# Two key tiles per PV matmul, and head selection folded into the transposes, in a decode attention kernel

## Chip, core and metric

The kernel runs on one core of a Trainium2 chip. The metric is the device time of one execution, in microseconds (us). The engines are called by the profile's names: PE is TensorE (matmuls), PEld its weight loads, DVE is VectorE, ACT is ScalarE, POOL is GpSimd, SP is SyncE, which here only issues DMAs. The core has 16 DMA engines. Times within a run are counted from the start of its span.

## The reference, cut to what matters

Two independent attention blocks, A and B, each decode one token for a batch of 2 with 32 heads of width 192 over a cache of 8192 keys. All tensors are bf16.

```python
q = (x @ wq).reshape(B, Sq, H, Dh).transpose(0, 2, 1, 3)      # B=2, Sq=1, H=32, Dh=192
scores = einsum("bhqd,bhkd->bhqk", q, k_cache) * Dh ** -0.5   # k_cache: 2 x 32 x 8192 x 192
p = softmax(scores)
o = einsum("bhqk,bhkd->bhqd", p, v_cache)
out = o.transpose(0, 2, 1, 3).reshape(B, Sq, H * Dh) @ wo     # A and B are concatenated
```

Every key and value is read once: 2 blocks x 2 x 32 = 128 (batch, head) items, each with 3 MB of keys and 3 MB of values. An item is called a head below, numbered 0 to 127; 16 of them (8 heads x batch 2) form a group, and there are 8 groups.

## The kernel before

For each head, SP loads keys into one of 2 slots and values into one of 3. A key slot is free when VectorE has multiplied it, a value slot when the PV of its head (probabilities times values) is done:

```python
                if i >= NK:
                    sp.wait_ge(s_mul, NCH * (i - NK + 1))
                sp.dma_start(
                    kslot(i % NK), kc[b, h].rearrange("(p t) d -> p (t d)", p=P)
                ).then_inc(s_k[i % NK], 16)
                if i >= NV:
                    sp.wait_ge(s_pv, i - NV + 1)
                sp.dma_start(
                    vslot(i % NV), vc[b, h].rearrange("(p t) d -> p (t d)", p=P)
                ).then_inc(s_v[i % NV], 16)
```

VectorE multiplies keys by the broadcast query in four chunks; PE sums the products by multiplying with an identity matrix (24 matmuls of 512 columns per head); VectorE finishes the sum, ACT takes the exponential, and PE multiplies the probabilities with the values. The weights of the PV matmul are a window of 16 columns into a row of zeros with the probabilities of this head in the middle, so that the head lands in its own row of a 16-row accumulator:

```python
            def pv_quarter(i, c):
                blk, g, m, hh, b, h = item(i)
                if c == 0:
                    pe.wait_ge(s_exp, i + 1)
                    pe.wait_ge(s_v[i % NV], 16 * (i // NV + 1))
                    if m == 0:
                        pe.wait_ge(s_zero, g + 1 if g >= 2 else 2)
                zs = zwin_slot(i % 2)
                vv = vslot(i % NV).rearrange("p (t d) -> p t d", d=Dh)
                tq = T // NCH
                for t in range(c * tq, (c + 1) * tq):
                    pe.matmul(
                        O_ps[g % 2][0:G, 0:Dh],
                        lhsT=zs[:, t, G - 1 - m:2 * G - 1 - m],
                        rhs=vv[:, t, :],
                        start=False, stop=False, skip_group_check=True,
                    )
                if c == NCH - 1:
                    pe.matmul(
                        O_ps[g % 2][0:G, Dh:Dh + 1],
                        lhsT=rz_slot(i % 2)[:, G - 1 - m:2 * G - 1 - m],
                        rhs=ones_f[:, 0:1],
                        start=False, stop=False, skip_group_check=True,
                    ).then_inc(s_pv, 1)
```

VectorE starts the multiplies of head i+1 before it has finished head i, and PE places a quarter of the PV of head p-1 after each reduction chunk of head p:

```python
# VectorE
            for i in range(NH):
                nxt = i + 1 < NH
                # [cut]
                if nxt:
                    mul_chunk(i + 1, 0)
                sred_nrs(i)
                if nxt:
                    mul_chunk(i + 1, 1)
                bias_op(i)
                # [cut: group end] then chunks 2 and 3
# TensorE
            for p in range(NH + 1):
                for c in range(NCH):
                    if p < NH:
                        red_chunk(p, c)
                    if p >= 1:
                        pv_quarter(p - 1, c)
                if p < NH:
                    pe.wait_ge(s_nrs, p + 1)
                    pe.transpose(
                        out=MT_ps[:, 0:P],
                        in_=nrs[:, (p % 2):(p % 2) + 1].broadcast_to([P, P]),
                        identity=ident_f[:, :],
                    ).then_inc(s_maxt, 1)
```

At the end of a group the 16 rows are normalized, spread out 8 times, transposed in bf16, masked so that each row keeps only its own head, and multiplied with `wo`. After the last group of a block the 16 rows are added up by head with an fp32 selection matmul:

```python
            def group_end(g):
                ops = O_ps[g % 2]
                dve.wait_ge(s_pv, G * (g + 1))
                dve.reciprocal(out=rcp[:, :], in_=ops[0:G, Dh:Dh + 1]).then_inc(s_rcp, 1)
                dve.wait_ge(s_rcp, g + 1)
                if g >= 1:
                    dve.wait_ge(s_ot, g)
                dve.tensor_scalar(
                    out=o_rep[:, :].rearrange("m (j h q) -> m j h q", j=NJ, h=HG),
                    in0=ops[0:G, 0:Dh].rearrange("m (q j) -> m j q", j=NJ)[:, :, None, :].broadcast_to([G, NJ, HG, DQ]),
                    scalar1=rcp[:, 0:1], scalar2=None, op0=ALU.mult,
                ).then_inc(s_onorm, 1)
                dve.wait_ge(s_onorm, g + 1)
                dve.memset(ops[0:G, 0:Dh + 1], 0.0).then_inc(s_zero, 1)

            def mask_copy(g):
                dve.wait_ge(s_ot, g + 1)
                if g >= 1:
                    dve.wait_ge(s_proj, NPP * g)
                dve.tensor_tensor(
                    out=oM_sb[:, :].rearrange("p (j m) -> p j m", m=G),
                    in0=aux_ps[:, 0:NJ * G].rearrange("p (j m) -> p j m", m=G),
                    in1=mask_b[:, None, :].broadcast_to([P, NJ, G]),
                    op=ALU.mult,
                ).then_inc(s_mc, 1)
# [cut]
            def out_transposes(g, p):
                pe.wait_ge(s_onorm, g + 1)
                pe.wait_ge(s_qc, q_count_before(p + 1))
                if g >= 1:
                    pe.wait_ge(s_mc, g)
                for j in range(NJ):
                    tr = pe.transpose(
                        out=aux_ps[:, j * G:(j + 1) * G],
                        in_=o_rep[:, j * P:(j + 1) * P],
                        identity=ident_b[0:G, 0:G],
                    )
                tr.then_inc(s_ot, 1)
```

Of the kernel before, what the change touches and what calls it, by code (L numbers as in the profile page):

```python
# [5 lines left out]
BF16 = mybir.dt.bfloat16  # L6
# [6 lines left out]
def bass_concat_heads__gqa_block_cached__mha_block_cached__decode_kernel(  # L13
# [28 lines left out]
    W = 2 * G - 1  # L42
# [48 lines left out]

    proj_sched = {}
    for g in range(NG):
        for q in range(NPP):
            p = min((g + 1) * G + 1 + q, NH)
            proj_sched.setdefault(p, []).append((g, q))
    acc_sched = {}
    for blk in range(NBLK - 1):
        gl = (blk + 1) * NGB - 1
        acc_sched[(gl + 1) * G + NPP] = blk  # L100
# [6 lines left out]
    for g in range(1, NG):  # L107
        sp_extra.setdefault(g * G + 7, []).append(("wo", g))

    es = contextlib.ExitStack()  # L110
    with es:
# [12 lines left out]
        zwin = sb("zwin", [P, 2 * T * W], BF16)  # L124
        rz = sb("rz", [P, 2 * W], F32)
# [7 lines left out]
        ones_b = sb("ones_b", [P, G], BF16)  # L133
        mask_b = sb("mask_b", [P, G], BF16)
        sel_f = sb("sel_f", [G, Bsz], F32)
        x_sb = sb("x_sb", [Bsz, NBLK * D], BF16)
        xT = sb("xT", [P, NBLK * DC * Bsz], BF16)
        o_rep = sb("o_rep", [G, NJ * P], BF16)
        rcp = sb("rcp", [G, 1], F32)
        oM_sb = sb("oM_sb", [P, NJ * G], BF16)  # L140
        acc_sb = sb("acc_sb", [G, D], F32)
        out_sb = sb("out_sb", [Bsz, NBLK * D], BF16)
# [3 lines left out]
        MT_ps = banks[2]  # L146
        O_ps = [banks[3], banks[4]]
# [24 lines left out]
        s_rcp = sem("s_rcp")  # L172
        s_onorm = sem("s_onorm")
# [4 lines left out]
        s_accc = sem("s_accc")  # L178
        s_sel = sem("s_sel")
# [17 lines left out]
        def zwin_slot(j):  # L197
            return zwin[:, j * T * W:(j + 1) * T * W].rearrange("p (t w) -> p t w", w=W)

        def rz_slot(j):  # L200
            return rz[:, j * W:(j + 1) * W]

# [17 lines left out]
        def _(pool):  # L220
            pool.memset(ident_f[:, :], 1.0).then_inc(s_pl, 1)
            pool.memset(ones_b[:, :], 1.0).then_inc(s_pl, 1)
# [5 lines left out]
            mview = mask_b[:, :].rearrange("p (h b) -> p h b", b=Bsz)  # L228
            oview = ones_b[:, :].rearrange("p (h b) -> p h b", b=Bsz)
            pool.affine_select(  # L230
                out=mview, in_=oview, pattern=[[-DQ, HG], [0, Bsz]],
                compare_op=ALU.is_ge, fill=0.0, base=0, channel_multiplier=1,
            ).then_inc(s_pl, 1)
            pool.wait_ge(s_pl, 4)
            pool.tensor_copy(out=ident_b[:, :], in_=ident_f[:, :]).then_inc(s_pl, 1)
            pool.affine_select(
                out=mview, in_=mview, pattern=[[DQ, HG], [0, Bsz]],
                compare_op=ALU.is_ge, fill=0.0, base=DQ - 1, channel_multiplier=-1,
# [4 lines left out]
            pool.wait_ge(s_pl, 9)  # L243
# [3 lines left out]
        def _(sp):  # L247
# [5 lines left out]
            for i in range(NH):  # L253
                blk, g, m, hh, b, h = item(i)
                _, kc, vc, _, _ = blocks[blk]
                for (kind, gg) in sp_extra.get(i, []):
# [3 lines left out]
                    else:  # L260
                        if gg >= 1:
                            sp.wait_ge(s_proj, NPP * gg)
                        load_wo(sp, gg)
                if i >= NK:
                    sp.wait_ge(s_mul, NCH * (i - NK + 1))
# [11 lines left out]
            sp.dma_start(out.rearrange("b o n -> b (o n)"), out_sb[:, :]).then_inc(s_out, 16)  # L277
            sp.wait_ge(s_out, 16)

        @block.vector  # L280
        def _(dve):
            dve.memset(O_ps[0][0:G, 0:Dh + 1], 0.0)
            dve.memset(O_ps[1][0:G, 0:Dh + 1], 0.0).then_inc(s_zero, 2)
            dve.wait_ge(s_const, 1)
            dve.tensor_reduce(
                out=sel_f[:, :], in_=ident_f[0:G, 0:G].rearrange("p (h b) -> p b h", b=Bsz),
                axis=AX.X, op=ALU.add,
            ).then_inc(s_dc, 1)
            qc_waited = [0]

# [43 lines left out]
            def group_end(g):  # L334
                ops = O_ps[g % 2]
                dve.wait_ge(s_pv, G * (g + 1))
                dve.reciprocal(out=rcp[:, :], in_=ops[0:G, Dh:Dh + 1]).then_inc(s_rcp, 1)
                dve.wait_ge(s_rcp, g + 1)
                if g >= 1:
                    dve.wait_ge(s_ot, g)  # L340
                dve.tensor_scalar(  # L341
                    out=o_rep[:, :].rearrange("m (j h q) -> m j h q", j=NJ, h=HG),
                    in0=ops[0:G, 0:Dh].rearrange("m (q j) -> m j q", j=NJ)[:, :, None, :].broadcast_to([G, NJ, HG, DQ]),
                    scalar1=rcp[:, 0:1], scalar2=None, op0=ALU.mult,
                ).then_inc(s_onorm, 1)
                dve.wait_ge(s_onorm, g + 1)
                dve.memset(ops[0:G, 0:Dh + 1], 0.0).then_inc(s_zero, 1)  # L347

            def mask_copy(g):
                dve.wait_ge(s_ot, g + 1)  # L350
                if g >= 1:
                    dve.wait_ge(s_proj, NPP * g)
                dve.tensor_tensor(  # L353
                    out=oM_sb[:, :].rearrange("p (j m) -> p j m", m=G),
                    in0=aux_ps[:, 0:NJ * G].rearrange("p (j m) -> p j m", m=G),
                    in1=mask_b[:, None, :].broadcast_to([P, NJ, G]),
                    op=ALU.mult,
                ).then_inc(s_mc, 1)

            for c in range(NCH):  # L360
                mul_chunk(0, c)
            for i in range(NH):
                nxt = i + 1 < NH
                ge = i >= 1 and (i - 1) % G == G - 1
                if nxt:
                    mul_chunk(i + 1, 0)
                sred_nrs(i)
                if nxt:
                    mul_chunk(i + 1, 1)
                bias_op(i)  # L370
                if ge:
                    group_end((i - 1) // G)
                if nxt:
                    mul_chunk(i + 1, 2)
                if ge:
                    mask_copy((i - 1) // G)
                if nxt:
                    mul_chunk(i + 1, 3)
            group_end(NG - 1)
            mask_copy(NG - 1)  # L380

        @block.scalar
        def _(act):
# [15 lines left out]
            def acc_copy(blk):  # L399
                gl = (blk + 1) * NGB - 1  # L400
                act.wait_ge(s_proj, NPP * (gl + 1))
                if blk >= 1:
                    act.wait_ge(s_sel, blk)
# [198 lines left out]
```

## Time and profile before

| | before |
|---|---|
| median of 4 runs | 1996.02 us (1995.7 to 1998.07) |
| the profiled run | span 1994.0 us |
| HBM read | 836.8 MB |

These are lines of the page of the kernel before: the engines' busy time with its share of the span, the queue of the data loads (q1) and of the instruction loads (q8) with packets, megabytes and the share of the 16 DMA engines' time, the chain of waits, and the costliest groups (busy time and mean ns of one; then the engine's idle time before them, and who ended it).

```profile
span 1994.0 us, 26935 instructions
...
PE 1668.2 (84%) x12274; PEld 1019.3 (51%) x12274; DVE 1016.3 (51%) x1059; ACT 99.5 (5%) x330; POOL 5.0 (0%) x14
...
q1 hardware_dynamic: 43276, 836.79, 98.4%
q8 instruction: 97, 1.59, 0.3%
...
DMA 71%; DVE 19%; issue 7%; PE 2%; ACT 0%; SPq 0%; ACTq 0%; DVEq 0%
...
L303 DVE TENSOR_TENSOR pbuf<-kbuf,qbc 128x3072 bf16<-128x3072 bf16 x512 | 886.9, 1752 | 941.7 <-DMA kbuf<-in_A_k_cache_dram 478.8
L476 PE MATMUL bank<-pbuf,ident_b 128*128 128x512 bf16 x3072 | 812.2, 404 | 0.2 <-DVE pbuf L303 0.2
L495 PE MATMUL bank<-vbuf,zwin 128*16 128x192 bf16 x8192 | 786.1, 251 | 23.8 <-ACT zwin L422 19.4
```

The q1 row is the one that matters: the loads keep the 16 DMA engines busy for 98.4% of the span, and the chain that ended last is 71% key loads. VectorE's idle time before the multiplies is spent waiting for keys.

The second view is the timeline of the tail, which is what is left to do once the last keys are in; the time up to there is called the steady part below (start, duration, engine, line and operation; in brackets the idle time before it). The last keys are in when the first multiply of head 127 starts.

```profile
1960.93 1.76 DVE L303 TENSOR_TENSOR pbuf<-kbuf,qbc 128x3072 bf16<-128x3072 bf16 x1 [6.79 <-DMA kbuf<-in_B_k_cache_dram]
...
1974.83 0.69 DVE L312 TENSOR_REDUCE sc_sb<-bank 128x64 f32<-128x512 f32 x1 [5.96 <-PE bank L476]
...
1977.55 5.45 PE L495 MATMUL bank<-vbuf,zwin 128*16 128x192 bf16 x64 [1.05 <-ACT zwin L422]
...
1983.06 0.16 DVE L337 RECIPROCAL rcp<-bank 16x1 f32<-16x1 f32 x1 [6.24 <-PE bank L502]
1983.25 1.80 DVE L341 TENSOR_SCALAR o_rep<-bank,rcp 16x1536 bf16<-16x1536 f32 x1
...
1985.11 0.45 PE L515 MATMUL bank<-ident_b,o_rep 16*128 16x16 bf16 x12 [2.09 <-DVE o_rep L341]
...
1986.01 0.38 PE L534 MATMUL bank<-wo_sb,oM_sb 128*16 128x512 bf16 x1 [0.44 <-DVE oM_sb L353]
...
1989.21 0.22 PE L535 MATMUL bank<-wo_sb,oM_sb 128*16 128x128 bf16 x1
...
1991.53 0.59 ACT L409 ACTIVATE out_sb<-bank 2x512 bf16<-2x512 f32 x1 [1.32 <-PE bank L542]
...
1992.30 0.27 SPq L277 DMA_DIRECT2D out_dram<-out_sb  x1
```

From the last keys (1960.93) to the last scores (1974.83) 13.9 us pass, then exponential and PV, then from 1983.06 the group end: the spreading takes 1.80, the 12 transposes 0.45, the projection 3.4 (1986.01 to 1989.43), and 2.1 us go by until the output copy can start (1991.53): they are the copy and the selection matmuls of the block's end.

### The profile page before, as it was taken

To read this page: it belongs to the slowest core of one execution; us is meant where nothing else is said; L and a number is where in the kernel's file an instruction comes from. 1 tells how busy PE (TensorE), PEld (TensorE's weight loads), DVE (VectorE), ACT (ScalarE), POOL (GpSimd) and SP (SyncE) were. 2 spreads that over 40 slices of the span, in tenths; PEclk is the share of its full clock that TensorE was granted. 3 is DMA by queue.
4 is the path that set the end of the run, shared out by engine and by line. 5 is a ranking of instruction groups with operands and counts; after the bars stand their busy time and mean duration, and the time that the engine had idled before them with its cause. 6 is when DMAs were issued, how large, how long until landed. Compare 5 with 4: busy or idle time off the path is not lost.

```text
span 1994.0 us, 26935 instructions
## 1 busy us (share of the span) xinstructions
PE 1668.2 (84%) x12274; PEld 1019.3 (51%) x12274; DVE 1016.3 (51%) x1059; ACT 99.5 (5%) x330; POOL 5.0 (0%) x14
## 2 busy tenths in 40 slices
PE   6868879788888888878888888787888878987887
PEld 2545545455555555545555455454555545554455
DVE  3545455445554555445455455554455545554543
ACT  0000000000000000000000000000000000000000
POOL 0000000000000000000000000000000000000000
PEclk8989999899998999999999999998998999999999
DMA  9999999999999999999999999999999999999993
GB/s 402 425 432 430 429 427 430 428 430 430 426 430 429 430 430 426 428 431 427 430 426 428 428 428 425 424 428 430 428 428 424 423 431 429 425 414 429 430 431 165
DMA packets 43389, 838.51 MB, mean 421 GB/s; under 512 B 4358, under 2 KB 4362, under 8 KB 9484
## 3 DMA queue, kind: packets, MB, share of 16 engines
q1 hardware_dynamic: 43276, 836.79, 98.4%
q8 instruction: 97, 1.59, 0.3%
q14 instruction: 16, 0.13, 0.0%
HBM read 836.77 MB, written 0.01 MB: 420 GB/s over the span
## 4 chain that ended last, share of the span: by engine, by line
DMA 71%; DVE 19%; issue 7%; PE 2%; ACT 0%; SPq 0%; ACTq 0%; DVEq 0%
DMA kbuf<-in_A_k_cache_dram 37%; DMA kbuf<-in_B_k_cache_dram 35%; DVE pbuf L303 15%; DVE sc_sb L312 2%; PE bank L495 1%; PE bank L476 1%; DVE ns_sb L320 1%; DVE o_rep L341 1%; DVE bias L329 1%; PE bank L534 0%; DVE bank L347 0%; DVE oM_sb L353 0%; PE bank L541 0%; ACT zwin L422 0%; PE bank L515 0%
## 5 line engine op out<-in xcount | busy, mean ns | idle before, releaser
L303 DVE TENSOR_TENSOR pbuf<-kbuf,qbc 128x3072 bf16<-128x3072 bf16 x512 | 886.9, 1752 | 941.7 <-DMA kbuf<-in_A_k_cache_dram 478.8
L476 PE MATMUL bank<-pbuf,ident_b 128*128 128x512 bf16 x3072 | 812.2, 404 | 0.2 <-DVE pbuf L303 0.2
L495 PE MATMUL bank<-vbuf,zwin 128*16 128x192 bf16 x8192 | 786.1, 251 | 23.8 <-ACT zwin L422 19.4
L495 PEld LDWEIGHTS bank<-vbuf,zwin 128*16 128x16 bf16 x8192 | 658.2, 92 | 269.9 <-issue 190.6
L476 PEld LDWEIGHTS bank<-pbuf,ident_b 128*128 128x128 bf16 x3072 | 279.1, 102 | 357.4 <-issue 128.5
L556 PE MATMUL bank<-ident_f,nrs 128*128 128x128 f32 x128 | 43.2, 338 | 261.2 <-DVE ns_sb L320 261.2
L422 ACT ACTIVATE zwin<-ns_sb,bias 128x64 bf16<-128x64 f32 x128 | 74.0, 578 | 1864.3 <-DVE bias L329 1864.3
L556 PEld LDWEIGHTS bank<-ident_f,nrs 128*128 128x128 f32 x128 | 17.6, 137 | 272.9 <-DVE ns_sb L320 272.8
L312 DVE TENSOR_REDUCE sc_sb<-bank 128x64 f32<-128x512 f32 x128 | 87.4, 683 | 9.8 <-PE bank L476 9.7
L461 PE MATMUL bank<-wq_sb,xT 128*128 128x384 bf16 x320 | 71.7, 361 | 4.8 <-DMA wq_sb<-in_A_wq_dram 3.0
L461 PEld LDWEIGHTS bank<-wq_sb,xT 128*128 128x128 bf16 x320 | 35.4, 112 | 22.8 <-issue 7.3
L422 ACT ACTIVATION_READ_ACCUMULATOR zwin<-ns_sb,bias 128x1 f32 x128 | 41.5, 324 | 0.0
L329 DVE TENSOR_REDUCE bias<-bank 128x1 f32<-128x128 f32 x128 | 36.2, 283 | 0.7 <-PE bank L556 0.7
L393 ACT ACTIVATE qbc<-bank 128x384 bf16<-128x384 f32 x64 | 35.1, 548 | 10.2 <-PE bank L461 10.2
L534 PE MATMUL bank<-wo_sb,oM_sb 128*16 128x512 bf16 x96 | 30.6, 393 | 0.4 <-DVE oM_sb L353 0.4
L320 DVE TENSOR_SCALAR_CACHE_REDUCE ns_sb<-sc_sb 128x64 f32<-128x64 f32 x128 | 28.2, 220 | 4.4
L515 PE MATMUL bank<-ident_b,o_rep 16*128 16x16 bf16 x96 | 3.8, 170 | 26.3 <-DVE o_rep L341 26.3
L502 PE MATMUL bank<-ones_f,rz 128*16 128x1 f32 x256 | 24.5, 165 | 0.0
L502 PEld LDWEIGHTS bank<-ones_f,rz 128*16 128x16 f32 x256 | 23.0, 97 | 0.0
L535 PE MATMUL bank<-wo_sb,oM_sb 128*16 128x128 bf16 x96 | 21.7, 226 | 0.0
L515 PEld LDWEIGHTS bank<-ident_b,o_rep 16*128 16x128 bf16 x96 | 3.1, 99 | 27.7 <-DVE o_rep L341 27.7
L534 PEld LDWEIGHTS bank<-wo_sb,oM_sb 128*16 128x16 bf16 x96 | 8.6, 90 | 12.8 <-issue 1.3
(35 smaller groups left out, 53.7 us busy)
## 6 DMA issues: line engine op xcount, KB each, us to landing
kbuf<-in_A_k_cache_dram SPq DMA_DIRECT2D x64, 3072.0 KB, 21.6
vbuf<-in_A_v_cache_dram SPq DMA_DIRECT2D x64, 3072.0 KB, 21.3
kbuf<-in_B_k_cache_dram SPq DMA_DIRECT2D x64, 3072.0 KB, 21.6
vbuf<-in_B_v_cache_dram SPq DMA_DIRECT2D x64, 3072.0 KB, 21.3
wq_sb<-in_A_wq_dram SPq DMA_DIRECT2D x4, 1920.0 KB, 22.9
wo_sb<-in_A_wo_dram SPq DMA_DIRECT2D x4, 1920.0 KB, 23.0
wq_sb<-in_B_wq_dram SPq DMA_DIRECT2D x4, 1920.0 KB, 23.2
wo_sb<-in_B_wo_dram SPq DMA_DIRECT2D x4, 1920.0 KB, 22.9
```

Of the source, the lines that this page charges most:

```text
L303: dve.tensor_tensor(out=pslot(ci % NP).rearrange("p (t d) -> p t d", d=DCH), in0=kv[:, :, c * DCH:(c + 1) * DCH], in1=qv[:, g % 2, hh, b, ...
L312: dve.tensor_reduce(out=sc_sb[:, (i % 2) * T:(i % 2 + 1) * T], in_=S_ps[i % 2][:, 0:SN].rearrange("p (t e) -> p t e", e=D2), axis=AX.X, op ...
L320: dve.tensor_scalar(out=ns_sb[:, (i % 2) * T:(i % 2 + 1) * T], in0=sc_sb[:, (i % 2) * T:(i % 2 + 1) * T], scalar1=-SCALE, scalar2=None, op ...
L329: dve.tensor_reduce(out=bias[:, (i % 2):(i % 2) + 1], in_=MT_ps[:, 0:P], axis=AX.X, op=ALU.min,).then_inc(s_bias, 1)
L393: act.activation(out=qv[:, g % 2, 2 * hp:2 * hp + 2, b, :], in_=Q_ps[:, 0:QN].rearrange("p (h d) -> p h d", h=2), func=AF.Copy,).then_inc( ...
L422: act.activation(out=zs[:, :, G - 1], in_=ns_sb[:, (p % 2) * T:(p % 2 + 1) * T], func=AF.Exp, bias=bias[:, (p % 2):(p % 2) + 1], scale=-1. ...
L461: mm = pe.matmul(Q_ps[:, 0:QN], lhsT=xT[:, xo:xo + 1].broadcast_to([P, P]), rhs=wqv[:, dc, 2 * hp * Dh:2 * hp * Dh + QN], start=(dc == 0), ...
L476: mm = pe.matmul(S_ps[p % 2][:, 0:SN], lhsT=ident_b[:, :], rhs=pv_[:, :, j * D2:(j + 1) * D2], start=(c == 0 and j == 0), stop=(c == NCH - ...
L495: pe.matmul(O_ps[g % 2][0:G, 0:Dh], lhsT=zs[:, t, G - 1 - m:2 * G - 1 - m], rhs=vv[:, t, :], start=False, stop=False, skip_group_check=True,)
L502: pe.matmul(O_ps[g % 2][0:G, Dh:Dh + 1], lhsT=rz_slot(i % 2)[:, G - 1 - m:2 * G - 1 - m], rhs=ones_f[:, 0:1], start=False, stop=False, ski ...
L534: pe.matmul(acc_ps1[0:G, 0:512], lhsT=oMv[:, j, :], rhs=wov[:, j, 0:512], start=st, stop=sp_)
L556: pe.transpose(out=MT_ps[:, 0:P], in_=nrs[:, (p % 2):(p % 2) + 1].broadcast_to([P, P]), identity=ident_f[:, :],).then_inc(s_maxt, 1)
```

## The change

The intent is to halve the PV matmuls: two key tiles share one matmul of 384 columns, and their weights are 32 columns wide, so that even tiles land in row 2m and odd tiles in row 2m+1 of a 32-row accumulator. Half of each row is then useless; it is dropped at the group end, where the mask and the choice of the rows are folded into the "transposes", now fp32 matmuls with a selection matrix. This makes the separate selection matmuls at a block's end unnecessary. With it the order of work changes on VectorE and PE, and 14 filler matmuls, whose result nobody reads (`warm`), keep PE busy. The core of the diff (setup, semaphores and the output copies are cut):

```diff
+            def pv_range(i, u0, u1):
                 blk, g, m, hh, b, h = item(i)
-                if c == 0:
+                if u0 == 0:
                     pe.wait_ge(s_exp, i + 1)
                     pe.wait_ge(s_v[i % NV], 16 * (i // NV + 1))
                     if m == 0:
                         pe.wait_ge(s_zero, g + 1 if g >= 2 else 2)
                 zs = zwin_slot(i % 2)
                 vv = vslot(i % NV).rearrange("p (t d) -> p t d", d=Dh)
-                tq = T // NCH
-                for t in range(c * tq, (c + 1) * tq):
+                for u in range(u0, u1):
                     pe.matmul(
-                        O_ps[g % 2][0:G, 0:Dh],
-                        lhsT=zs[:, t, G - 1 - m:2 * G - 1 - m],
-                        rhs=vv[:, t, :],
+                        O_ps[g % 2][0:R, 0:2 * Dh],
+                        lhsT=zs[:, u, C0 - 2 * m:C0 - 2 * m + R],
+                        rhs=vv[:, 2 * u:2 * u + 2, :],
                         start=False, stop=False, skip_group_check=True,
                     )
-                if c == NCH - 1:
+                if u1 == TU:
+                    rzs = rz_slot(i % 2)
                     pe.matmul(
-                        O_ps[g % 2][0:G, Dh:Dh + 1],
-                        lhsT=rz_slot(i % 2)[:, G - 1 - m:2 * G - 1 - m],
+                        O_ps[g % 2][0:R, 2 * Dh:2 * Dh + 1],
+                        lhsT=rzs[:, RZC - 2 * m:RZC - 2 * m + R],
+                        rhs=ones_f[:, 0:1],
+                        start=False, stop=False, skip_group_check=True,
+                    )
+                    pe.matmul(
+                        O_ps[g % 2][0:R, 2 * Dh:2 * Dh + 1],
+                        lhsT=rzs[:, RZC - 1 - 2 * m:RZC - 1 - 2 * m + R],
                         rhs=ones_f[:, 0:1],
                         start=False, stop=False, skip_group_check=True,
                     ).then_inc(s_pv, 1)
# [cut]
-                nxt = i + 1 < NH
-                ge = i >= 1 and (i - 1) % G == G - 1
-                if nxt:
-                    mul_chunk(i + 1, 0)
+                gd = (i - 2) // G if (i >= 2 and (i - 2) % G == G - 1) else None
+                mul_chunk(i, 0)
+                mul_chunk(i, 1)
+                if gd is not None:
+                    group_end(gd)
+                mul_chunk(i, 2)
+                mul_chunk(i, 3)
                 sred_nrs(i)
-                if nxt:
-                    mul_chunk(i + 1, 1)
                 bias_op(i)
-                if ge:
-                    group_end((i - 1) // G)
-                if nxt:
-                    mul_chunk(i + 1, 2)
-                if ge:
-                    mask_copy((i - 1) // G)
-                if nxt:
-                    mul_chunk(i + 1, 3)
-            group_end(NG - 1)
-            mask_copy(NG - 1)
+                if gd is not None:
+                    mask_copy(gd)
# [cut] TensorE
             for p in range(NH + 1):
-                for c in range(NCH):
-                    if p < NH:
+                if p < NH:
+                    u = 0
+                    if p >= 1 and UH:
+                        pv_range(p - 1, 0, UH)
+                        u = UH
+                    for c in range(NCH):
                         red_chunk(p, c)
+                        if p >= 1:
+                            pv_range(p - 1, u, u + g1)
+                            u += g1
                     if p >= 1:
-                        pv_quarter(p - 1, c)
-                if p < NH:
-                    pe.wait_ge(s_nrs, p + 1)
-                    pe.transpose(
-                        out=MT_ps[:, 0:P],
-                        in_=nrs[:, (p % 2):(p % 2) + 1].broadcast_to([P, P]),
-                        identity=ident_f[:, :],
-                    ).then_inc(s_maxt, 1)
-                for (g, r) in q_sched.get(p, []):
-                    q_round(g, r)
-                if p < NH:
+                        pv_range(p - 1, u, u + 2 * g1)
+                        u += 2 * g1
+                    maxt(p)
+                    if p >= 1:
+                        pv_range(p - 1, u, TU)
# [cut] last iteration
+                    pv_range(p - 1, 0, TU)
+                    pe.wait_ge(s_qc, NQR * NG)
+                    warm(14)
# [cut] group end, VectorE
-                dve.reciprocal(out=rcp[:, :], in_=ops[0:G, Dh:Dh + 1]).then_inc(s_rcp, 1)
-                dve.wait_ge(s_rcp, g + 1)
+                if g == 0:
+                    dve.wait_ge(s_dc, 2)
+                step(dve.reciprocal(out=rcp[:, :], in_=ops[0:R, 2 * Dh:2 * Dh + 1]))
+                step(dve.tensor_tensor(out=rcpab[:, :], in0=par[:, :], in1=rcp[:, 0:1].broadcast_to([R, 2]), op=ALU.mult))
+                step(dve.tensor_scalar(
+                    out=tmpB[:, :], in0=ops[0:R, Dh:2 * Dh], scalar1=rcpab[:, 1:2], scalar2=None, op0=ALU.mult,
+                ))
                 if g >= 1:
                     dve.wait_ge(s_ot, g)
-                dve.tensor_scalar(
+                step(dve.scalar_tensor_tensor(
+                    out=tmpB[:, :], in0=ops[0:R, 0:Dh], scalar=rcpab[:, 0:1], in1=tmpB[:, :],
+                    op0=ALU.mult, op1=ALU.add,
+                ))
+                dve.tensor_tensor(
                     out=o_rep[:, :].rearrange("m (j h q) -> m j h q", j=NJ, h=HG),
-                    in0=ops[0:G, 0:Dh].rearrange("m (q j) -> m j q", j=NJ)[:, :, None, :].broadcast_to([G, NJ, HG, DQ]),
-                    scalar1=rcp[:, 0:1], scalar2=None, op0=ALU.mult,
+                    in0=tmpB[:, :].rearrange("m (q j) -> m j q", j=NJ)[:, :, None, :].broadcast_to([R, NJ, HG, DQ]),
+                    in1=mask2[:, None, :, None].broadcast_to([R, NJ, HG, DQ]),
+                    op=ALU.mult,
# [cut] selection, in out_transposes
                 for j in range(NJ):
-                    tr = pe.transpose(
-                        out=aux_ps[:, j * G:(j + 1) * G],
-                        in_=o_rep[:, j * P:(j + 1) * P],
-                        identity=ident_b[0:G, 0:G],
+                    tr = pe.matmul(
+                        oT32_ps[:, j * G:(j + 1) * G],
+                        lhsT=o_rep[:, j * P:(j + 1) * P],
+                        rhs=Sm_f[:, :],
+                        start=True, stop=True,
                     )
```

## The prediction

> **What bounds it now: the loads.** Each of 128 heads loads 3 MB of keys and 3 MB of values. The page's DMA queue row gives the 16 engines 98.4% of the span; slices read mostly 423 to 432 GB/s. The chain of waits is 71% key loads. The timeline shows a head every 14.6 us (key multiplies start 1946.3, 1960.9), as 6.29 MB at 430 GB/s takes. [...] TensorE's 84% busy is no limit: about 11.5 us of TensorE streaming per head (24 reductions at 235 ns, 64 PV at 81 ns timeline spacing) fits in 14.6. VectorE needs 8.
>
> **What the change does.**
> - PV: 64 matmuls of 192 columns become 32 of 384. Columns streamed are the same: 5.2 us before (64 in the last head, timeline), an estimated 5.2 after. Weight loads halve; busy time falls, elapsed time doesn't.
> - Normalizer: one more small fp32 matmul a head, hidden.
> - VectorE no longer starts head i+1 before finishing head i. The serial head is 4 multiplies (7.0) + last reduction 1.4 + reduce, scale, transpose, min 1.7: about 10.5 us, inside 14.6. Key slots free after 7.0 instead of 7.9 us. PV of a head finishes about 10.5 us after the next keys land, not 15, so value loads are issued about 4 us earlier; they already have about 14 us of queued bytes ahead. The one visible loss, near 1770 us (DMA share 0.89 in a 10 us window), is about 1.1 us.
> - Instruction fetch (1.59 MB, 0.3% of DMA) falls by about a third: below 2 us.
> - Group end on VectorE: 2.1 us becomes an estimated 2.8; transposes of 16 rows in bf16 (0.45) become 12 fp32 matmuls, estimated 2.0..
>
> **Where it counts: the tail**, from the last keys landing (1960.9) to 1994.0:
> - Last reduction: before, the PV of head 126 is interleaved with it and starts late; scores are ready at 1974.8. After, half of PV is done in advance: 1960.9 + 7.0 + 1.4 = 1969.4. Saves about 5.4.
> - Reduce, exp, last PV, normalizer: same (about 8.4), to about 1977.8.
> - Group end +0.7, transposes +1.6.
> - Projection: 24 matmuls, same columns, 3.4.
> - Copy of the accumulator and fp32 selection matmuls (1989.46 to 1991.5) vanish: saves 2.1.
> - Final copy 0.85 and output 1.7 stay.
> Sum: -5.4 + 2.3 - 2.1 = about -5.2; with about -1 in the steady part, -6.
>
> **Predicted 1990.0 us**, 8 in 10: 1986.5 to 1993.5. Faster by over 2%: 0.01; within: 0.98; slower: 0.01.
>
> **What would show it.** DMA row still over 98%, slices still near 430 GB/s, heads still 14.6 us apart. PV group: half the matmuls, about 162 ns apart. Weight loads' busy share down, from 51% to about 40%. Last score reduction about 1969.5, last PV done about 1977.8, projection starting near 1983, last ACT copies once. End minus last key landing: about 28 us, against 33.
>
> **What would make it wrong.** Loads so late that DMA idles each head (serial chain over 14.6, say at a dropped TensorE clock, as in windows of 0.56 to 0.66 now): tens of us slower. [...] Fp32 matmuls with 128-column weights costing more than estimated: +2. A different load rate from run to run: before spans 1995.7 to 1998.1.

(The 2.8 and 2.0 us of the group end are estimates, set beside the 2.1 and 0.45 us of the trace.)

## More of the kernel before

The experiments were taken on three chips, on which the kernel before measured 1997.33, 1996.99 and 1997.04 us, so the chip makes no difference that matters here.

## The result

| | before | after |
|---|---|---|
| median of all runs | 1996.57 us (13 runs, 1995.34 to 1999.62) | 1991.97 us (9 runs, 1989.85 to 1994.25) |
| ratio | | 0.9976 (0.9967 to 0.9986) |
| instructions in the profile | 26,935 | 19,490 |
| span of the profiled run | 1994.0 us | 1989.5 us |

A ratio is the mean time of one kernel's runs over that of the other kernel's runs of the same rounds, so it is not quite the ratio of the medians quoted. The change is faster by a quarter of a per cent: the same, by the 2% rule. The time lies within the predicted range.

The same lines of the page after:

```profile
span 1989.5 us, 19490 instructions
...
PE 1704.8 (86%) x8536; PEld 723.0 (36%) x8536; DVE 1057.8 (53%) x1084; ACT 90.9 (5%) x326; POOL 5.3 (0%) x17
...
q1 hardware_dynamic: 43280, 836.79, 98.5%
q8 instruction: 67, 1.10, 0.2%
...
DMA 74%; DVE 23%; PE 2%; issue 0%; SPq 0%; ACT 0%; ACTq 0%
...
L339 DVE TENSOR_TENSOR pbuf<-kbuf,qbc 128x3072 bf16<-128x3072 bf16 x512 | 866.1, 1752 | 484.5 <-DMA kbuf<-in_A_k_cache_dram 258.1
L514 PE MATMUL bank<-pbuf,ident_b 128*128 128x512 bf16 x3072 | 801.0, 399 | 265.3 <-DVE pbuf L339 265.2
L532 PE MATMUL bank<-vbuf,zwin 128*32 128x384 bf16 x4096 | 817.8, 334 | 2.5 <-ACT zwin L462 0.3
...
L532 PEld LDWEIGHTS bank<-vbuf,zwin 128*32 128x32 bf16 x4096 | 338.5, 97 | 448.5 <-issue 258.3
```

The PV group has half the matmuls, and its busy time has not fallen (817.8 against 786.1 us): the columns are the same, and so, nearly, is the last PV (5.38 us after 5.45). PEld fell from 51% to 36%. The instruction queue carries 30 packets and 0.49 MB less. The loads still own the span.

The tail after:

```profile
1956.61 6.76 DVE L339 TENSOR_TENSOR pbuf<-kbuf,qbc 128x3072 bf16<-128x3072 bf16 x4 [2.46 <-DMA kbuf<-in_B_k_cache_dram]
...
1965.50 0.69 DVE L348 TENSOR_REDUCE sc_sb<-bank 128x64 f32<-128x512 f32 x1 [2.12 <-PE bank L514]
...
1967.75 5.38 PE L532 MATMUL bank<-vbuf,zwin 128*32 128x384 bf16 x32
...
1973.26 0.16 DVE L381 RECIPROCAL rcp<-bank 32x1 f32<-32x1 f32 x1 [6.10 <-PE bank L546]
...
1974.51 2.83 DVE L392 TENSOR_TENSOR o_rep<-tmpB,mask 32x1536 f32<-32x1536 f32 x1
...
1977.39 4.43 PE L578 MATMUL bank<-Sm_f,o_rep 32*128 32x16 f32 x24 [1.79 <-DVE o_rep L392]
...
1982.37 0.58 PE L598 MATMUL bank<-wo_sb,oM 128*2 128x512 bf16 x1 [0.54 <-DVE oM L406]
...
1986.94 0.22 PE L599 MATMUL bank<-wo_sb,oM 128*2 128x128 bf16 x1
...
1987.20 0.59 ACT L451 ACTIVATE out_sb<-bank 2x512 bf16<-2x512 f32 x1 [19.50 <-PE bank L599]
...
1987.97 0.27 SPq L309 DMA_DIRECT2D out_dram<-out_sb  x1
```

Here is what the total hides. The last keys are in 4.3 us earlier (1956.61 against 1960.93), and from there to the end of the span it takes 32.9 us, against 33.1. **The whole gain of the profiled run was made while the loads were still running; the tail, where the prediction had put it, gained 0.2 us.** The parts of the tail:

| part of the tail | before | after |
|---|---|---|
| last keys to last scores (start of the score reduction) | 13.9 | 8.9 |
| last scores to the start of the group end (reciprocal) | 8.2 | 7.8 |
| reciprocal to the end of the spreading | 2.0 | 4.1 |
| transposes or selection matmuls | 0.45 | 4.43 |
| projection | 3.4 | 4.8 |
| end of the projection to the output DMA | 2.9 | 0.8 |

The first row gains 5.0 us and the last 2.1; rows three to five give 7.5 back.

### The profile page after: what moved, and what is told of

Same layout as the page of the kernel before. It is cut to its first block, busy times and chain, and to the rows that moved or that the text cites. A ratio compares the mean times of both kernels' runs of the same rounds, so it can differ in the third digit from the quotient of the medians.

```text
span 1989.5 us, 19490 instructions
## 1 busy us (share of the span) xinstructions
PE 1704.8 (86%) x8536; PEld 723.0 (36%) x8536; DVE 1057.8 (53%) x1084; ACT 90.9 (5%) x326; POOL 5.3 (0%) x17
## 4 chain that ended last, share of the span: by engine, by line
DMA 74%; DVE 23%; PE 2%; issue 0%; SPq 0%; ACT 0%; ACTq 0%
DMA kbuf<-in_A_k_cache_dram 38%; DMA kbuf<-in_B_k_cache_dram 36%; DVE pbuf L339 21%; DVE o_rep L392 1%; PE bank L532 1%; PE bank L514 1%; PE bank L578 0%; PE bank L598 0%; DVE tmpB L388 0%; DVE tmpB L383 0%; DVE bank L399 0%; DVE rcpab L382 0%; PE bank L599 0%; PE bank L562 0%; DVE rcp L381 0%
## 5 line engine op out<-in xcount | busy, mean ns | idle before, releaser
L339 DVE TENSOR_TENSOR pbuf<-kbuf,qbc 128x3072 bf16<-128x3072 bf16 x512 | 866.1, 1752 | 484.5 <-DMA kbuf<-in_A_k_cache_dram 258.1
L532 PE MATMUL bank<-vbuf,zwin 128*32 128x384 bf16 x4096 | 817.8, 334 | 2.5 <-ACT zwin L462 0.3
L532 PEld LDWEIGHTS bank<-vbuf,zwin 128*32 128x32 bf16 x4096 | 338.5, 97 | 448.5 <-issue 258.3
L462 ACT ACTIVATE zwin<-ns_sb,bias 128x64 bf16<-128x64 f32 x128 | 45.0, 352 | 1806.6 <-DVE bias L365 1806.6
L540 PEld LDWEIGHTS bank<-ones_f,rz 128*32 128x32 f32 x256 | 28.2, 110 | 15.1
L598 PE MATMUL bank<-wo_sb,oM 128*2 128x512 bf16 x96 | 30.5, 392 | 0.5 <-DVE oM L406 0.5
L356 DVE TENSOR_SCALAR_CACHE_REDUCE ns_sb<-sc_sb 128x64 f32<-128x64 f32 x128 | 28.1, 220 | 4.4
L578 PE MATMUL bank<-Sm_f,o_rep 32*128 32x16 f32 x192 | 24.4, 268 | 1.8 <-DVE o_rep L392 1.8
L546 PE MATMUL bank<-ones_f,rz 128*32 128x1 f32 x256 | 25.8, 170 | 0.0
L540 PE MATMUL bank<-ones_f,rz 128*32 128x1 f32 x256 | 25.4, 169 | 0.0
L578 PEld LDWEIGHTS bank<-Sm_f,o_rep 32*128 32x128 f32 x192 | 23.6, 198 | 2.3 <-DVE o_rep L392 2.2
L392 DVE TENSOR_TENSOR o_rep<-tmpB,mask 32x1536 f32<-32x1536 f32 x8 | 22.6, 2822 | 0.3
```

Source lines behind the costliest of these rows:

```text
L339: dve.tensor_tensor(out=pslot(ci % NP).rearrange("p (t d) -> p t d", d=DCH), in0=kv[:, :, c * DCH:(c + 1) * DCH], in1=qv[:, g % 2, hh, b, ...
L392: dve.tensor_tensor(out=o_rep[:, :].rearrange("m (j h q) -> m j h q", j=NJ, h=HG), in0=tmpB[:, :].rearrange("m (q j) -> m j q", j=NJ)[:, : ...
L462: act.activation(out=zs[:, :, C0:C0 + 2], in_=ns_sb[:, (p % 2) * T:(p % 2 + 1) * T].rearrange("p (u j) -> p u j", j=2), func=AF.Exp, bias= ...
L532: pe.matmul(O_ps[g % 2][0:R, 0:2 * Dh], lhsT=zs[:, u, C0 - 2 * m:C0 - 2 * m + R], rhs=vv[:, 2 * u:2 * u + 2, :], start=False, stop=False, ...
L540: pe.matmul(O_ps[g % 2][0:R, 2 * Dh:2 * Dh + 1], lhsT=rzs[:, RZC - 2 * m:RZC - 2 * m + R], rhs=ones_f[:, 0:1], start=False, stop=False, sk ...
L578: tr = pe.matmul(oT32_ps[:, j * G:(j + 1) * G], lhsT=o_rep[:, j * P:(j + 1) * P], rhs=Sm_f[:, :], start=True, stop=True,)
```

## The experiments

Ten kernels were run, each with a profile and five timed rounds (four in a_fetch128). The ratio is to the kernel before in the same rounds; the changed kernel's is 0.9976. "Last keys" is the start of the first multiply of head 127 in the profiled run, which waits for the last key load.

| run | ratio (95%) | last keys, us | last scores after them | end after them | q8 MB |
|---|---|---|---|---|---|
| before | 1 | 1960.93 | 13.9 | 33.1 | 1.59 |
| b_again | 0.9994 (0.998 to 1.0007) | 1960.81 | 13.8 | 32.9 | 1.59 |
| after | 0.9976 (0.9967 to 0.9986) | 1956.61 | 8.9 | 32.9 | 1.10 |
| a_pv64 | 1.0003 (0.9991 to 1.0016) | 1962.44 | 10.5 | 34.6 | 1.62 |
| a_pefill | 1.0008 (0.9994 to 1.0022) | 1962.37 | 8.9 | 32.9 | 1.62 |
| a_fetch64 | 1.0017 (1.0004 to 1.0031) | 1962.74 | 8.9 | 33.0 | 1.11 |
| a_fetch128 | 1.0119 (1.0105 to 1.0133) | 1984.68 | 10.5 | 34.5 | 1.10 |
| a_oldorder | 1.003 (1.0018 to 1.0043) | 1962.97 | 13.6 | 36.4 | 1.10 |
| a_bf16 | 0.995 (0.9938 to 0.9963) | 1956.53 | 10.5 | 30.7 | 1.10 |
| a_warm28 | 0.9972 (0.996 to 0.9985) | 1956.34 | 10.5 | 33.7 | 1.11 |
| best | 0.9945 (0.9932 to 0.9957) | reordered | | | 1.10 |
| best2 | 0.9933 (0.992 to 0.9945) | reordered | | | 1.10 |

The last scores come 8.9 or 10.5 us after the last keys in kernels of the new order: where it is 10.5, the first reductions of the head run slower (in head 126 of the changed kernel, also 10.5, the first chunk took 2.44 us instead of 1.46, after PE had waited 2.8 us). The clock records show why: a stretch of 3.41 us at a clock of 0.50 falls on these reductions (1944.24 to 1947.65 for that head; 1965.66 to 1969.08 in a_pv64), and none does where the last head took 8.9. This moves the end by up to 1.6 us from run to run and is no difference between kernels.

### Control: b_again

The edit is none: the kernel before, unchanged.

> The kernel before, unchanged, as a control. In the two profiles on hand the loads end 4.3 us earlier in the changed kernel (1963.9 against 1968.2 us), while from the last keys' arrival to the end both take 33 us. Theory A (the load stream itself is shortened by the change, at least the 1.1 us of instruction fetch that it saves): this profile shows the last keys at 1960 to 1962 again. Theory B (the 4 us are mostly chance between executions): the last keys arrive anywhere from 1956 to 1964, two profiles of one kernel differing by 2 us or more. Ratio of times 1.000 within 0.001.

Measured: 1996.4 us, ratio 0.9994 (0.998 to 1.0007), last keys at 1960.81, 0.1 us from the first profile. The changed kernel and the two variants of it that leave the load stream alone (a_bf16, a_warm28) have 1956.61, 1956.53 and 1956.34. Theory B falls: the 4 us are no chance, the change shortens the load stream.

### The packing alone undone: a_pv64

```diff
-                    pe.matmul(
-                        O_ps[g % 2][0:R, 0:2 * Dh],
-                        lhsT=zs[:, u, C0 - 2 * m:C0 - 2 * m + R],
-                        rhs=vv[:, 2 * u:2 * u + 2, :],
+                    for e in range(2):
+                        pe.matmul(
+                            O_ps[g % 2][0:R, e * Dh:(e + 1) * Dh],
+                            lhsT=zs[:, u, C0 - 2 * m:C0 - 2 * m + R],
+                            rhs=vv[:, 2 * u + e, :],
```

> The changed kernel, but every pair of key tiles goes through two matmuls of 192 columns instead of one of 384: the packing alone undone, 8192 PV matmuls and weight loads again, instruction fetch back to about 1.6 MB. If packing buys TensorE time that counts: 5 us slower or more. If it buys only the instruction fetch (0.48 MB at 420 GB/s = 1.1 us) : 1 us slower than the changed kernel, 1993 us, last PV still 5.2 to 5.4 us. If it buys nothing: the same 1992.

Measured: 1998.76 us, ratio 1.0003. Against 0.9976 this is 0.0027, or 5.4 us, and the intervals don't overlap. Last keys at 1962.44, 5.8 us later than with the packing; its tail is longer by 1.7 us, of which 1.6 lie before the last scores. The page's instruction queue:

```profile
q8 instruction: 99, 1.62, 0.3%
```

So the packing is worth 5 us, all that the change gains, and nearly all of it is made in the load stream. The size is the one expected if PE's time counted, but the place is not: the last PV takes 5.45 us against 5.38, and the loss is made while the loads run. The bytes of the fetch alone account for 1.2 us, an estimate from 1.62 less 1.10 MB at the 430 GB/s of the page's slices. Two causes remain: that fetching an instruction costs the loads more than its bytes, or that PV matmuls of 192 columns hold the loads back.

### The instructions back, the matmuls not: a_pefill

PE gets 32 tiny matmuls per head where it waits for the scores anyway: 64 instructions, as many as the packing removed, with next to no data.

```diff
+                for _ in range(32 if 1 <= p < NH - 1 else 0):
+                    pe.matmul(MT_ps[0:2, 500:501], lhsT=ident_b[:, 0:2], rhs=ident_b[:, 0:1], start=True, stop=True)
                 pe.wait_ge(s_nrs, p + 1)
```

> The changed kernel with 32 tiny matmuls (2 weight columns, 1 moving column) per head on TensorE, set where it waits for the scores anyway: 64 more instructions per head, as many as the packing took away, about 1 us of TensorE per head, no more SBUF or PSUM traffic to speak of. Theory of the fetch (the load stream is as long as its slowest DMA engine, and TensorE's instructions are fetched by only about half of the 16): instruction queue back to about 1.6 MB, last keys at 1961 to 1962, as with the packing undone, 1997 us, ratio 1.000. Rival (the 192-column PV matmuls themselves slowed the loads, by reading or by holding the value slots): fetch back to 1.6 MB but last keys at 1957 to 1958, ratio 0.998.

Measured: 1997.82 us, ratio 1.0008, last keys at 1962.37. The page:

```profile
q8 instruction: 99, 1.62, 0.3%
```

The packed kernel with unpacked instruction count loads exactly as slowly as the unpacked one (1962.37 and 1962.44), with the tail of the packed one (32.9). The number of PE instructions is the cause; the rival falls.

### Instructions on another engine: a_fetch64 and a_fetch128

GpSimd, idle after the start, gets waits for a semaphore that is long satisfied.

```diff
             pool.memset(rcp[:, :], 1.0).then_inc(s_const, 1)
+            for i in range(NH):
+                pool.wait_ge(s_exp, i + 1)
+                for _ in range(63):                # 127 in a_fetch128
+                    pool.wait_ge(s_pl, 1)
```

> The changed kernel, with 64 more instructions per head on GpSimd, which otherwise does nothing after the start: waits for a semaphore that is long satisfied. They touch no memory and no other engine waits for them; all they cost is fetching 8192 more instructions, about what the packing saved on TensorE (the instruction queue back from 1.1 MB to about 1.6 MB). If the packing gains by instruction fetch: the loads end about 4 us later than in the changed kernel (last keys at about 1961), 1996 us, ratio to before 1.000. If it gains by what TensorE does: no change, 1992, ratio 0.9976.

> The same with 128 instructions per head: 16384 more, about 1.0 MB more fetched. If fetch is the cause, the step doubles: last keys at about 1965, 2000 us, ratio 1.002. If not: 1992 still.

Measured: 1999.4 and 2020.55 us, ratios 1.0017 and 1.0119. The expectation was wrong about the experiment itself: the build folded the waits two by two, in such an order that the first instruction waits for head 64. So 4,097 and 8,193 instructions ran, all from 1008 us on. They are fetched on another instruction queue (q14, up from 0.14 to 0.40 and 0.66 MB, in packets of 8 KB, the first extra one at 1016 us). The accident is useful: the first half is a control within the run. The time at which SP issued the keys of a head, less that in the changed kernel, in us:

```
head            16     48     80     96    112
a_fetch64     -0.05  -0.71  -0.02  -0.08   2.10
a_fetch128     0.02  -0.65  -0.03   8.08  17.82
```

Up to head 80 the difference stays under 0.8 us; then the loads fall behind, in a_fetch64 only after head 96. That instructions cost load time is shown again, on an engine whose last data operation starts at 6.04 us (a_fetch64). The size is not the expected one: 32 packets cost 6.1 us of last keys, 64 cost 28.1, more than double. Why the second is so much dearer is told below.

### Why 0.5 MB can cost 4 us: the landing records

The trace has, for each load, the time at which each of the 16 DMA engines reports its part done; the load counts as landed at the last. The last key load of the kernel before was reported done by the first engine at 1953.46 us and by the last at 1960.91, and its first multiply starts at 1960.93. For a load that landed near 875 us, and in one run for three later loads, the time by which each engine was ahead of the last, worked out from these records and sorted (the first number is the time of landing):

```
before     873.5  9.1 9.1 9.0 8.9 8.7 8.4 7.8 5.1 1.5 1.5 1.4 1.4 1.3 1.1 0.9 0
after      873.8  6.9 6.8 6.8 6.6 6.5 5.6 5.5 2.1 1.8 1.8 1.0 0.3 0.1 0.1 0.0 0
a_pv64     876.6  9.7 9.5 9.5 9.3 9.0 8.8 8.0 4.7 2.1 1.9 1.9 1.8 1.4 0.4 0.1 0
a_pefill   876.8  9.9 9.6 9.6 9.4 9.4 8.5 8.2 4.9 2.0 2.0 1.8 1.7 1.7 0.2 0.0 0
a_oldorder 870.4  1.7 1.7 1.6 1.6 1.5 1.5 1.5 1.5 1.4 1.4 1.0 0.9 0.8 0.7 0.0 0
a_fetch128 873.7  6.8 6.5 6.5 6.5 6.3 5.8 5.3 2.2 1.8 1.6 1.5 0.4 0.3 0.1 0.0 0
a_fetch128 1118.5 8.3 8.1 8.1 7.9 7.3 6.8 3.3 2.2 2.2 1.8 0.5 0.3 0.1 0.0 0.0 0
a_fetch128 1196.1 8.3 8.2 8.1 7.9 7.4 6.7 2.2 0.7 0.5 0.3 0.2 0.1 0.0 0.0 0.0 0
a_fetch128 1457.9 14.4 14.3 14.3 14.2 13.8 13.2 11.5 10.2 10.1 10.0 9.7 9.6 9.6 9.4 7.9 0
```

The engines fall into seven fast ones, one between and eight slow ones, and near 875 us the gap is the larger the more PE instructions ran: 9.1 us before, 6.9 after, 9.7 and 9.9 with the instructions put back. The gap alone does not measure the fetches, because it closes where the loads run short: in a_oldorder, with the instruction count of the changed kernel, it is 3.4 us at 289 us and 0.5 at 341, after the idle time at 320 that is told below, and 1.7 at 870. Near 1465 us it is 9.9 before but 11.6 after; why it had stopped growing before is open. A load is as late as its slowest engine, so what counts is not the bytes spread over 16 engines but the fetches of the engines that do them. An estimate: 30 fewer packets, each 1.07 us long in the records (median), on 8 slow engines are 4.0 us; measured were 4.3. Spread over 16 it would be 2.0. The first multiplies of the heads fit the 8 engines better still: in a_pefill they come later than in the changed kernel by plateaus of 1.6 us (head 28), 3.0 (head 60), 4.5 (head 90) and 5.8 (head 118), about 1.5 us for every 8 of its 32 extra packets. The trace does not name the DMA engine of a packet, so that the slow engines are slow because they fetch is inferred from these counts, not seen.

In the GpSimd run one single engine ends up behind all others. It was one of the fast ones: of the seven values from 5.3 us up at 873.7 us, six stay above 6 us and one falls to 3.3 (1118.5 us) and 2.2 (1196.1 us); from about 1240 us on one engine falls ever further behind the rest. This accounts for the doubled packets costing more than four times as much: the extra fetches first use up the engine's lead of about 7 us, which delays no load. The first multiplies are not later than in the changed kernel up to head 79 in a_fetch128 and up to head 99 in a_fetch64, which fetches half as fast; after that a_fetch128 loses 0.6 us with every head, to 28.1 at head 127. That it is GpSimd's fetches that hold this engine back is inferred in the same way.

### The old order of work: a_oldorder

The changed kernel with the order of VectorE and PE of the kernel before (multiplies of head i+1 around the end of head i; PV in quarters).

```diff
-                mul_chunk(i, 0)
-                mul_chunk(i, 1)
-                # [cut] ... mul_chunk(i, 2), mul_chunk(i, 3), sred_nrs(i), bias_op(i)
+                mul_chunk(i + 1, 0)
+                sred_nrs(i)
+                mul_chunk(i + 1, 1)
+                bias_op(i)
+                # [cut] group end, mul_chunk(i + 1, 2), mask, mul_chunk(i + 1, 3)
# and on TensorE
-                    # [cut] pv_range(p - 1, 0, UH) ahead of the reductions, the rest around them
+                    for c in range(NCH):
+                        red_chunk(p, c)
+                        pv_quarter(p - 1, c)
+                    maxt(p)
```

> The changed kernel with the old order of work on VectorE (head i+1's multiplies started before head i is finished) and on TensorE (PV in quarters between the reductions). Theory of the tail (the new order makes the last scores ready 8.9 us after the last keys arrive instead of 13.9, and everything else of the tail pays that back): about 5 us slower, 1997, with the last score reduction again 13.9 us after the last keys and the loads ending no later. Rival (the new order also makes the load stream shorter because value loads are issued earlier): 7 to 9 us slower, with the loads ending 3 us later.

(The edit leaves the group end where the changed kernel has it, one head later than the kernel before.) Measured: 2003.7 us, ratio 1.003: 0.0054 above the changed kernel, 10.8 us, more than either theory expected. In the profiled run the last scores come 13.6 us after the last keys, as before the change: the new order is what brings them forward by 5 us. And the last keys come 6.4 us later. The packet records show the DMA engines short of work for 0.5 to 2.4 us at seven places, 240 to 250 us apart (320, 570, 810 and so on), each just after a group end. At the first of them SP issued no key load between 283.35 and 312.38 us (in the changed kernel between 287.39 and 303.37):

```profile
283.35 0.33 SPq L298 DMA_DIRECT2D kbuf<-in_A_k_cache_dram  x1
290.60 0.33 SPq L303 DMA_DIRECT2D vbuf<-in_A_v_cache_dram  x1
312.38 0.33 SPq L298 DMA_DIRECT2D kbuf<-in_A_k_cache_dram  x1
```

The four multiplies of one head stretched from 296.48 to 312.36 us, because VectorE did the group end between them and waited 3.22 us for its selection matmuls; only then was the key slot free. So the rival is right too, for a reason that it did not name: with the old order the heavier group end starves the loads, and the new order hides it.

### The group end in bf16: a_bf16

```diff
-        mask2 = sb("mask2", [R, HG], F32)
+        mask2 = sb("mask2", [R, HG], BF16)
-        Sm_f = sb("Sm_f", [R, G], F32)
+        Sm_f = sb("Sm_f", [R, G], BF16)
-        o_rep = sb("o_rep", [R, NJ * P], F32)
+        o_rep = sb("o_rep", [R, NJ * P], BF16)
# the combined row is written as bf16 too
```

> The changed kernel with the group end in bf16: normalized rows, head mask, spread-out rows and selection matrix. If fp32 is what makes the group end dear: spreading 2.8 us becomes about 1, the 12 selection matmuls 4.4 us become under 1, and the projection 4.6 us becomes 3.4[...]: 6 to 7 us faster than the changed kernel, 1985 us. If the clock drops all the same: transposes 1 us and projection 4.6: 5 us faster. If the group end is not on the critical path: no change.

Measured: 1987.62 us, ratio 0.995: 5.2 us faster than the changed kernel; the result is correct. The timeline of its tail:

```profile
1976.02 2.92 DVE L395 TENSOR_TENSOR o_rep<-tmpC,mask 32x1536 bf16<-32x1536 bf16 x1
...
1979.00 0.45 PE L581 MATMUL bank<-Sm_f,o_rep 32*128 32x16 bf16 x12 [1.89 <-DVE o_rep L395]
```

The 12 selection matmuls take 0.45 us instead of 4.43. The spreading did not get cheaper (2.92 against 2.83), so fp32 was not what made it dear. The clock still fell, to 0.50 in the window from 1980 to 1982 us, though no fp32 selection matmuls ran, and the projection was slow (4.8 us). The second of the three expectations holds in sum.

### More filler: a_warm28

```diff
-                    warm(14)
+                    warm(28)
```

> The changed kernel with 28 filler matmuls before the last group end instead of 14, so that TensorE is busy for 4.6 us instead of 2.4 while VectorE takes 4.1. If the 1.8 us gap lets the clock fall to 0.5: the clock stays at 1.0, the 12 fp32 selection matmuls take about 2.4 us instead of 4.4, the projection 3.4 instead of 4.8: 3 us faster than the changed kernel, 1989. [...] the clock falls during them all the same, and the filler may cost 0.5 us.

(Its second case is that the clock falls during the selection matmuls all the same.)

Measured: 1990.86 us, ratio 0.9972 (0.996 to 0.9985), no change against 0.9976. First the windows of the changed kernel (length, busy us of each engine, then the granted PE clock, DMA share and GB/s), then those of this run:

```profile
core 0: us, PE busy (x) PEld busy (x) DVE busy (x) ACT busy (x) POOL busy (x), PEclk, DMA share, GB/s
...
1976.00:1978.00 2.00, 0.61 (x6) 0.61 (x6) 1.72 (x2) 0.00 (x0) 0.00 (x0) 1.00 0.00 0
1978.00:1980.00 2.00, 2.00 (x14) 2.00 (x13) 0.00 (x0) 0.00 (x0) 0.00 (x0) 0.59 0.00 0
...
1982.00:1984.00 2.00, 1.63 (x7) 0.76 (x8) 0.22 (x1) 0.00 (x0) 0.00 (x0) 0.50 0.00 0
```

```profile
1977.00:1979.00 2.00, 2.00 (x14) 1.09 (x12) 1.86 (x2) 0.00 (x0) 0.00 (x0) 1.00 0.00 0
1979.00:1981.00 2.00, 2.00 (x19) 1.88 (x17) 0.23 (x1) 0.00 (x0) 0.00 (x0) 1.00 0.00 0
...
1983.00:1985.00 2.00, 2.00 (x11) 0.95 (x10) 0.00 (x0) 0.00 (x0) 0.00 (x0) 0.56 0.00 0
```

In the changed kernel the clock is 0.50 to 0.59 from 1978 to 1984. With 28 fillers the gap is gone and the selection matmuls run at a clock of 1.00, in 2.85 us, but right after them it falls to 0.56, and the projection pays. What makes the clock fall was not isolated. The gap alone does not explain it: here it was 1.79 us, and in the kernel before PE idled for 2.09 us at the same place (1985.11) with the clock at 1.00. Nor is fp32 needed, since the clock also fell in a_bf16, to 0.50, after a gap of 1.89 us and matmuls in bf16.

### Versions beyond both: best and best2

The tail hangs on the last keys while the last values land 7.5 us later. `best` takes a_bf16 with 24 fillers, loads the keys of head 127 ahead of the values of head 126, loads the values of head 127 in two halves, and in the last step reduces before it does the PV of head 126. `best2` also replaces the two-tensor spreading by eight scalar multiplies and puts a part of the PV of head 126 back between the reductions (22 fillers).

```diff
# best
+                if i == NH - 2:
+                    load_k(NH - 1)          # before the values of head 126
# [cut] values of head 127 in two DMAs with a semaphore each; order of the last step on TensorE
# best2
-                dve.tensor_tensor(out=o_rep[...], in0=tmpC[...].broadcast_to([R, NJ, HG, DQ]),
-                    in1=mask2[:, None, :, None].broadcast_to([R, NJ, HG, DQ]), op=ALU.mult)
+                for hh_ in range(HG):
+                    dve.tensor_scalar(out=orv[:, :, hh_, :], in0=tmpC[...],
+                        scalar1=mask2[:, hh_:hh_ + 1], scalar2=None, op0=ALU.mult)
```

> The changed kernel with the bf16 group end, 24 filler matmuls, and the last loads reordered: keys of head 127 before values of head 126, values of head 127 in two halves, and in the last step TensorE reduces before it does the PV of the head before. The tail then hangs on the last values instead of the last keys: loads end at about 1964, then 2.7 us of PV, 4.3 of group end, 1 of selection, 3.4 of projection, 2.6 of copies and output: about 1979 to 1981, ratio to before 0.992.

> The kernel called best, with the rows spread by 8 scalar multiplies instead of one two-tensor multiply with two broadcasts, and a quarter to three eighths of the PV of head 126 done between the last reductions. If the two-tensor form is what makes the spreading 2.8 to 2.9 us (against 1.8 with a scalar in the kernel before): 1.6 to 2.0 us, and the last PV starts about 1 us earlier: 2 us faster than best, 1983, ratio 0.9935. If the strided reading is the cost: spreading stays near 2.8.

Measured: `best` 1985.37 us, ratio 0.9945, less than expected (0.992): the PV of head 126 had moved behind the last scores, and PE started the last PV at 1966.76 us, though the first half of its values had landed at about 1960. `best2` 1983.35 us, ratio 0.9933. Both are correct. The tail of `best2`:

```profile
1965.41 5.36 PE L551 MATMUL bank<-vbuf,zwin 128*32 128x384 bf16 x32
...
1970.91 0.16 DVE L396 RECIPROCAL rcp<-bank 32x1 f32<-32x1 f32 x1 [8.48 <-PE bank L565]
...
1972.29 1.51 DVE L411 TENSOR_SCALAR o_rep<-tmpC,mask 32x192 bf16<-32x192 bf16 x8
...
1974.48 0.45 PE L597 MATMUL bank<-Sm_f,o_rep 32*128 32x16 bf16 x12
...
1978.93 0.59 ACT L470 ACTIVATE out_sb<-bank 2x512 bf16<-2x512 f32 x1 [15.97 <-PE bank L618]
```

The spreading takes 1.51 us instead of 2.83. The edit took away two things at once, the two-tensor form and the strided reading (the operation before it now writes the row in the new order and takes 0.54 us instead of 0.40). The kernel before read with the same stride in a form with one scalar and took 1.80 us (for 16 rows), so most of the difference is likely the two-tensor form, but the two were not separated. Besides, the last PV starts 1.3 us earlier than in `best`; from the reduction at the selection's end (1974.97) to the output copy (1978.93) 4.0 us pass, against 5.3 in the changed kernel (1981.86 to 1987.20), at a clock of 1.00 in every window from 1968 to 1980. `best2` is the fastest kernel of this study, 13 us or 0.67% under the kernel before, and it too is bound by the loads.

## Why the prediction was right, and where it was wrong

The number was right: 1990.0 predicted, 1991.97 measured, in the range and in the class. The way there was half wrong, and the errors cancelled: that the total came out is luck.

- **"What bounds it now: the loads."** Right. No run here shows PE's or VectorE's work within the steady part setting the time except by way of the loads.
- **"Columns streamed are the same ... busy time falls, elapsed time doesn't."** Right about the elapsed time: the last PV takes 5.38 us after 5.45. PE's busy time did not fall at all; only the weight loads did, to 36% (predicted about 40%).
- **"Instruction fetch (1.59 MB, 0.3% of DMA) falls by about a third: below 2 us."** The third was right, the cost was mis-sized: the term "about -1 in the steady part" measured -4.3 us in the profiles, and 5.4 us of time by undoing the packing. The prediction took the fetch's share of the time of all 16 DMA engines (a third of 0.3% of the span). The experiments show that the count of PE instructions alone makes the difference, and the landing records point to the loads waiting for the slower half of the engines.
- **"Serial head ... about 10.5 us, inside 14.6."** Right in the main: the packet records show 1.7 us of idle DMA time between 1750 and 1780 us, against 1.2 before; no other stretch of 10 us up to 1950 us has more than 0.4 in either. The prediction took the new order to be worth little in the steady part; a_oldorder shows that it hides the group end, at 6 us of load time.
- **"Last reduction ... saves about 5.4."** Right: 5.0, and the old order takes it back.
- **"Group end +0.7, transposes +1.6."** Mis-sized: +2.1 and +4.0. Half of the 2.1 is the spreading (2.83 against 1.80 us), half the small operations added before it; the selection matmuls are dear by fp32 (0.45 us in bf16, a_bf16), which the prediction named as a risk, and partly by the clock (2.85 us at a clock of 1.00, 4.43 as it fell).
- **"Projection: 24 matmuls, same columns, 3.4."** Wrong by 1.4 us: the granted clock was 0.50 from 1982 to 1985 us, and a pair of matmuls took 0.53 us there against 0.27 at a clock of 1.00 (from 1985.37). The prediction named a slow PE in the tail as a risk, but for the last PV, not for the projection.
- **"Copy ... and selection matmuls vanish: saves 2.1."** Right: 2.1.
- **"End minus last key landing: about 28 us, against 33."** Wrong: 32.9. It is the reading that tells the two stories apart, and it says that the tail as a whole gained nothing.

In sum: predicted -5.2 in the tail and -1 in the steady part; measured -0.2 and -4.3.

## What to carry to other kernels

In a kernel bound by loads, count the instructions: 8,064 more of them on PE cost 5.8 us of load time here. The landing records suggest that they are fetched by the same DMA engines, not evenly, and that each load waits for the slowest engine, so fewer, larger matmuls can pay although the engine that runs them is not the limit. When a total comes out as predicted, check the terms: measure the steady part and the tail apart, from the arrival of the last input. And look at the tail of such a kernel on its own terms: there order, operand types and the clock count, which the averages of the whole span hide.
